# Moving the large SBUF buffers of an attention decode kernel to multiples of 4 KB

## Chip, cores and metric

The kernel runs on one core of one Trainium2 chip. The metric is the device time of one execution in microseconds.

## The reference, cut to what matters

One token, 32 query heads, 8 KV heads, 65536 cached keys of 128 dimensions, all bf16:

```python
q = (x @ wq) as 32 heads of 128
scores = einsum(q, k) * 128 ** -0.5        # k_cache, v_cache: [1, 8, 65536, 128]
o = einsum(softmax(scores), v)
h = x + o.reshape(1, 1, 4096) @ wo         # x is layer-normed before wq
h2 = h + (sigmoid(g) * u) @ w_down         # g, u = norm(h) @ w_gate, w_up (512 x 1792)
```

The two caches are 128 MB (MiB) each, so the kernel reads 282.33 MB (10^6 bytes) per call and computes little on each byte.

## The kernel before

K and V come in blocks of 4 MB: 128 partitions, one contiguous row of 32 KB for each. They land in four slots of one tensor, `ring`. VectorE transposes K from `ring` into `ktw`; TensorE makes scores from `ktw` and the output from the V slots. `ktw` is used again for `wo`, and the slots for the feed-forward weights. Allocation is in the order of the calls, from the bottom of SBUF up:

```python
SLOT = T * DH                                  # 16384 bf16 = 32 KB a partition
ring = sb("ring", [128, NSLOT * SLOT], bf16)   # the first tensor of the kernel
ktw = sb("ktw", [128, NKT * CH + WH], bf16)
P_sb = sb("P_sb", [128, 4 * 512], bf16)
# ... [cut: some 50 smaller tensors]

order = [("wq", 0)]
order += [("K", b) for b in range(NR)]
for b in range(NR, NB):
    order += [("K", b), ("V", b - NR)]
# ... [cut: the last V blocks and the weights]
for ld in order:
    k, b = ld
    s = slot_of[ld]
    dst = slot_ap(s)
    deps = [freed(prev[ld])]                   # the slot's last reader
    # ... [cut: weights]
    src = cache[0, h, r * BLK:(r + 1) * BLK, :].rearrange("(p t) d -> p (t d)", t=T)
    dma("sp", lambda e, d=dst, sr=src: e.dma_start(d, sr), ..., deps, f"{k}{b}")
```

In the built program some constants lie below `ring`, which therefore starts at byte 16512 of each partition; `ktw` starts at 147584. Both are 128 bytes past a multiple of 4096.

## Time and profile before

Median 660.75 us of 3 runs (660.71 to 660.75).

| what | value | where |
|---|---|---|
| load queue | 99.7% of the time of 16 DMA engines | page, queues |
| rate, 100 to 600 us | 432 GB/s | DMA view of that stretch |
| TensorE, VectorE busy | 64%, 53% | page, engines |
| 32 KB packets, 140 to 580 us | 1213 to 1224 ns, mean 1217.0 | the trace's DMA records |

The page of the kernel before:

```profile
span 659.3 us, 6111 instructions
PE 418.7 (64%) x2315; PEld 73.3 (11%) x1547; DVE 349.7 (53%) x439; ACT 42.9 (7%) x114; POOL 3.6 (1%) x17
...
DMA  9999999999999999999999999999999999999998
...
q1 hardware_dynamic: 10658, 282.33, 99.7%
...
DMA 36%; DVE 28%; PE 28%; issue 6%; ACT 1%; SPq 0%; DVEq 0%
...
L430 PE MATMUL PS<-ktw 128*128 128x512 bf16 x1024 | 298.2, 440 | 160.1 <-DVE ktw L510 156.3
L510 DVE STREAM_TRANSPOSE ktw<-ring 128x1024 f32<-128x1024 f32 x256 | 291.6, 1205 | 131.0 <-DMA ring<-in_A_k_cache_dram 131.0
...
ring<-in_A_k_cache_dram SPq DMA_DIRECT2D x32, 4096.0 KB, 29.3
ring<-in_A_v_cache_dram SPq DMA_DIRECT2D x31, 4096.0 KB, 26.9
```

The queue line (packets, MB, share) and the row of nines show DMA engines that never pause until the last slice. The chain of waits names VectorE and TensorE for over half of the span, but a load lands 27 to 29 us after its issue while 4 MB take 9.7 us at 432 GB/s: about three loads are queued at any time, and compute only decides when the next one joins (in the waits view the issues of loads, L364, wait 326.7 us for VectorE and 246.7 us for TensorE). VectorE's transposes wait 131 us in all for K to land.

The DMA view of the kernel before, 100 to 600 us (packets, MB and rate; then the load queue):

```profile
DMA packets 7408, 216.01 MB, mean 432 GB/s; under 512 B 816, under 2 KB 816, under 8 KB 816
...
q1 hardware_dynamic: 7408, 216.01, 100.4%
```

Over 100% means that the records of neighbouring packets of one engine overlap by a few ns. So the record's length is not quite the time a packet takes up. The better number is the period: 16 engines work side by side, and the start of the packet 16 places later, minus the start of this one, averaged over 140 to 580 us, is 1214.17 ns, 2.8 ns less than the mean record of 1217.0 ns. (The stretches given for packet records count from the trace's own zero, which lies about 11 us before the span that the views count from: 11.4 us in this run.)

### The profile page before, as it was taken

Reading aid. Unit: us, or ns where it says so; the run is one execution under the profiler, and the core shown is the slowest. Engines: PE = TensorE matmul, PEld = TensorE weight load, DVE = VectorE, ACT = ScalarE, POOL = GpSimd, SP = SyncE. Lnnn points to the kernel's source line nnn. Section 1 sums busy time; section 2 is a strip of 40 time slices with the busy share of each in tenths; the row PEclk is TensorE's granted clock in tenths of the full one; section 3 lists DMA queues with packets and bytes.
Section 4 is the critical chain, followed back from the end, with each engine's and each line's share of the span. In section 5 each row is a group of like instructions: output and inputs, shape, how many; then the busy total and the mean of one; then the engine's idle time right before and its main releaser. Section 6 shows DMA issues by size and latency. Waiting matters only on the chain.

```text
span 659.3 us, 6111 instructions
## 1 busy us (share of the span) xinstructions
PE 418.7 (64%) x2315; PEld 73.3 (11%) x1547; DVE 349.7 (53%) x439; ACT 42.9 (7%) x114; POOL 3.6 (1%) x17
## 2 busy tenths in 40 slices
PE   0688488548666585576765475764856668555846
PEld 0200011011000010010100110001100101001222
DVE  2299775547437665346555374465743565543202
ACT  1100200020000200020000200002000200002001
POOL 1000000000000000000000000000000000000000
PEclk9989699668887696776966779766878869667676
DMA  9999999999999999999999999999999999999998
GB/s 382 445 427 431 441 418 445 421 437 429 429 443 416 445 421 437 431 427 445 416 443 423 435 435 423 445 416 443 423 435 437 421 445 416 443 425 438 429 416 344
DMA packets 10802, 282.34 MB, mean 428 GB/s; under 512 B 1329, under 2 KB 1330, under 8 KB 1842
## 3 DMA queue, kind: packets, MB, share of 16 engines
q1 hardware_dynamic: 10658, 282.33, 99.7%
q10 hardware_dynamic: 144, 0.00, 0.0%
HBM read 282.33 MB, written 0.00 MB: 428 GB/s over the span
## 4 chain that ended last, share of the span: by engine, by line
DMA 36%; DVE 28%; PE 28%; issue 6%; ACT 1%; SPq 0%; DVEq 0%
DMA ring<-in_A_k_cache_dram 29%; PE PS L430 26%; DVE ktw L510 22%; DMA ring<-in_B_w_down_dram 4%; DVE M_sb L515 3%; DMA x_col<-in_A_x_dram 2%; DVE PT_sb L564 2%; ACT po_sb L598 1%; PE PS L548 1%; PE PS L541 1%; DVE gmj L543 0%; DVE gmrep L545 0%; PE PS L601 0%; PE PS L569 0%; DVE gm L539 0%
## 5 line engine op out<-in xcount | busy, mean ns | idle before, releaser
L430 PE MATMUL PS<-ktw 128*128 128x512 bf16 x1024 | 298.2, 440 | 160.1 <-DVE ktw L510 156.3
L510 DVE STREAM_TRANSPOSE ktw<-ring 128x1024 f32<-128x1024 f32 x256 | 291.6, 1205 | 131.0 <-DMA ring<-in_A_k_cache_dram 131.0
L430 PE MATMUL PS<-ring,PT_sb 128*32 x1024 | 83.2, 455 | 24.0 <-issue 13.5
L430 PEld LDWEIGHTS PS<-ktw 128*128 x256 | 26.9, 105 | 409.4 <-issue 256.5
L564 DVE STREAM_TRANSPOSE PT_sb<-P_sb 128x512 bf16<-128x512 bf16 x32 | 20.1, 684 | 53.5 <-PE PS L601 51.8
L550 ACT ACTIVATE negmax<-PS 128x1 f32<-128x1 f32 x8 | 1.4, 171 | 521.8 <-PE PS L548 521.8
L430 PEld LDWEIGHTS PS<-ring,PT_sb 128*32 x1024 | 25.4, 116 | 80.8 <-issue 76.1
L515 DVE TENSOR_REDUCE M_sb<-PS 128x1 f32<-128x512 f32 x32 | 19.9, 682 | 25.0 <-PE PS L430 25.0
L554 ACT ACTIVATE P_sb<-PS,negmax 128x512 bf16<-128x512 f32 x32 | 21.5, 685 | 0.3
L571 DVE TENSOR_REDUCE lsum<-PS 128x1 f32<-128x4 f32 x8 | 1.3, 162 | 29.9 <-PE PS L569 29.9
L541 PE MATMUL PS<-identf,gm 128*1 128x128 f32 x16 | 3.4, 301 | 16.9 <-DVE gm L539 16.9
L615 DVE TENSOR_TENSOR Lw<-O,blk_of 128x896 bf16<-128x896 bf16 (+1 forms) x2 | 1.4, 682 | 21.7 <-ACT O L605 21.7
L401 PE MATMUL PS<-st,onesf 128*128 128x2 f32 x4 | 1.2, 362 | 16.3 <-DVE st L400 16.3
L430 PE MATMUL PS<-ring,xz 128*8 x32 | 9.5, 470 | 2.3 <-issue 2.3
L598 ACT ACTIVATE po_sb<-PS,rl 128x512 bf16<-128x512 f32 x8 | 5.5, 687 | 53.6 <-PE PS L430 53.6
L430 PE MATMUL PS<-ktw,O 128*1 x26 | 7.5, 455 | 0.0
L548 PE MATMUL PS<-one_f,gmrep 1*128 1x1 f32 x16 | 4.2, 332 | 5.0 <-DVE gmrep L545 5.0
L475 DVE STREAM_TRANSPOSE qt<-qh 32x512 bf16<-32x512 bf16 x1 | 0.7, 700 | 11.0 <-ACT qh L472 11.0
L554 ACT ACTIVATION_READ_ACCUMULATOR P_sb<-PS,negmax 128x1 f32 x32 | 6.5, 203 | 0.0
L601 PE MATMUL PS<-sel_bf,po_sb 128*128 128x4 bf16 x32 | 2.1, 169 | 6.4 <-ACT po_sb L598 6.4
L416 DVE CAST hT<-x_col 128x4 f32<-128x4 bf16 x1 | 0.2, 170 | 10.8 <-DMA x_col<-in_A_x_dram 10.8
L660 DVE COPY yr<-PS 1x512 f32<-1x512 f32 x1 | 0.7, 679 | 8.1 <-PE PS L658 8.1
(82 smaller groups left out, 73.1 us busy)
## 6 DMA issues: line engine op xcount, KB each, us to landing
ring<-in_A_k_cache_dram SPq DMA_DIRECT2D x32, 4096.0 KB, 29.3
ring<-in_A_v_cache_dram SPq DMA_DIRECT2D x31, 4096.0 KB, 26.9
ring<-in_A_wq_dram SPq DMA_DIRECT2D x1, 4096.0 KB, 12.5
ktw<-in_A_wo_dram SPq DMA_DIRECT2D x1, 3584.0 KB, 13.3
ring<-in_A_v_cache_dram SPq DMA_DIRECT2D x1, 3072.0 KB, 13.2
ring<-in_B_w_gate_dram SPq DMA_DIRECT2D x1, 1792.0 KB, 19.1
ring<-in_B_w_up_dram SPq DMA_DIRECT2D x1, 1344.0 KB, 21.9
ring<-in_A_v_cache_dram SPq DMA_DIRECT2D x1, 1024.0 KB, 15.3
```

Of the source, the lines that this page charges most:

```text
L430: return e.add_instruction(mybir.InstMatmult(name=nc.get_next_instruction_name(), engine=mybir.EngineType.PE, ins=[rhs, lhsT], outs=[e.low ...
L510: op("dve", lambda e, d=dst, sr=src: e.transpose(d, sr), deps, f"T{b}.{c}", to="T")
L515: op("dve", lambda e, u=u: e.tensor_reduce(M_sb[:, u % 4:u % 4 + 1], ps(u % NS, 0, 512), AX.X, ALU.max), [f"S{b}.{NC - NR + k}"], f"mx{u}" ...
L541: op("pe", lambda e: e.matmul(ps(MISC, 0, 128, 0, 1), lhsT=gm[:, :], rhs=identf[:, :], start=True, stop=True), [f"gm{h}"], f"gmT{h}", to="Q")
L548: op("pe", lambda e: e.matmul(ps(MISC, 128, 129), lhsT=gmrep[0:1, :], rhs=one_f[0:1, 0:1], start=True, stop=True), [f"gmrep{h}"], f"neg{h}")
L550: op("act", lambda e: e.activation(negmax[:, k:k + 1], ps(MISC, 128, 129), AF.Copy, scale=-att_scale), [f"neg{h}"], f"negmax{h}")
L554: op("act", lambda e, b=b: e.activation(P_sb[:, (b % 4) * 512:(b % 4 + 1) * 512], ps(b % NS, 0, 512), AF.Exp, bias=negmax[:, k:k + 1], sca ...
L564: op("dve", lambda e, b=b: e.transpose(PT_sb[:, (b % 4) * 512:(b % 4 + 1) * 512], P_sb[:, (b % 4) * 512:(b % 4 + 1) * 512]), [f"E{b}", f"o ...
L571: op("dve", lambda e: e.tensor_reduce(lsum[:, :], ps(MISC, 132, 136), AX.X, ALU.add), [f"l{h}"], f"ls{h}", to="D")
L598: op("act", lambda e: e.activation(po_sb[:, :], ps(PO, 0, 512), AF.Copy, scale=rl[:, :]), [f"PV{NR * h + NR - 1}", f"rl{h}"], f"po{h}", to ...
L601: op("pe", lambda e, t=t: e.matmul(ps(OX, 0, 4), lhsT=po_sb[:, t * 128:(t + 1) * 128], rhs=sel_bf[:, 8 * t:8 * t + 8:2], start=(t == 0), s ...
L615: op("dve", lambda e: e.tensor_tensor(Lw[i][:, :].rearrange("p (j c) -> p j c", j=n), bass.AP(tensor=O2, offset=j0, ap=[[NQ, 128], [1, n], ...
```

## The change

The intent: the large DMA writes should start on a multiple of 4 KB in SBUF. Small tensors that came later now come first and fill the space up to byte 20480.

```diff
+        gsel = sb("gsel", [128, 128], fp32)
+        hz = sb("hz", [128, 128], fp32)
+        # ... [cut: 10 more small tensors, moved up from below]
+        blk_of = sb("blk_of", [128, 128 // RW], bf16)
         ring = sb("ring", [128, NSLOT * SLOT], bf16)
         ktw = sb("ktw", [128, NKT * CH + WH], bf16)
+        assert nc.lookup_mloc(ring).addr % 4096 == nc.lookup_mloc(ktw).addr % 4096 == 0
         P_sb = sb("P_sb", [128, 4 * 512], bf16)
         # ... [cut: the same small tensors taken out here and further down]
```

`ring` now starts at 20480 and `ktw` at 151552. Every engine has the same instructions in the same order.

More of the change, by code (lines that the diff above doesn't have):

```diff
@@ L236, in sb @@
             return es.enter_context(nc.sbuf_tensor(name, shape, dt))
+        gsel = sb("gsel", [128, 128], fp32)
+        hz = sb("hz", [128, 128], fp32)
+        identf = sb("identf", [128, 128], fp32)
+        onesf = sb("onesf", [128, 128], fp32)
+        lsel = sb("lsel", [128, 128], fp32)
+        iota_i = sb("iota_i", [128, 128], i32)
+        ident = sb("ident", [128, 128], bf16)
+        scr = sb("scr", [1, 64], fp32)
+        sel_f = sb("sel_f", [128, 32], fp32)
+        sel_bf = sb("sel_bf", [128, 32], bf16)
+        O2 = sb("O2", [128, NQ], bf16)
+        O3 = sb("O3", [128, NQ], bf16)
+        blk_of = sb("blk_of", [128, 128 // RW], bf16)
         ring = sb("ring", [128, NSLOT * SLOT], bf16)
         ktw = sb("ktw", [128, NKT * CH + WH], bf16)
+        assert nc.lookup_mloc(ring).addr % 4096 == nc.lookup_mloc(ktw).addr % 4096 == 0
         P_sb = sb("P_sb", [128, 4 * 512], bf16)
@@ L243, in bass_sequential_preLN__gqa_block_cached__glu_gated_glu__decode_kernel @@
         yr = sb("yr", [1, 512], fp32)
-        gsel = sb("gsel", [128, 128], fp32)
-        hz = sb("hz", [128, 128], fp32)
-        scr = sb("scr", [1, 64], fp32)
         po_sb = sb("po_sb", [128, 512], bf16)
-        O2 = sb("O2", [128, NQ], bf16)
-        ident = sb("ident", [128, 128], bf16)
-        identf = sb("identf", [128, 128], fp32)
-        onesf = sb("onesf", [128, 128], fp32)
-        lsel = sb("lsel", [128, 128], fp32)
-        iota_i = sb("iota_i", [128, 128], i32)
-        sel_f = sb("sel_f", [128, 32], fp32)
-        sel_bf = sb("sel_bf", [128, 32], bf16)
         one_f = sb("one_f", [1, 1], fp32)
@@ L284, in bass_sequential_preLN__gqa_block_cached__glu_gated_glu__decode_kernel @@
         W0 = NKT * CH
-        O3 = sb("O3", [128, NQ], bf16)
         Lw = [sb(f"Lw{i}", [128, n * DH // RW], bf16) for i, (_, n) in enumerate(WO)]
         row_of = sb("row_of", [128, RW], bf16)
-        blk_of = sb("blk_of", [128, 128 // RW], bf16)
         head_of = sb("head_of", [128, 4], fp32)
```

## The prediction

> **What bounds the kernel.** The DMA stream. The page's queue part shows the load queue busy for 99.7% of 16 engines' span, moving 282.33 MB; its engine part has PE at 64%, DVE at 53%, ACT at 7%. From 100 to 600 us the DMA view shows 432 GB/s and 100.4% busy (packets overlap by a few ns); K and V loads land a median 29.6 and 27.1 us after issue, about three 4 MB loads deep, so the queue never runs dry. The chain of waits is labelled DMA 36%, DVE 28%, PE 28%, but its DVE and PE steps run while loads are in flight; they pace the issues, not the bytes. Only about 2 us at the end (down-projection, cast, store) follow the last weight's landing.
>
> **What the change does.** Every engine runs the same instructions in the same order; only allocations move. In the built program the ring goes from byte 16512 to 20480 of each partition, the K-transpose/weight buffer from 147584 to 151552: both started 128 bytes past a multiple of 4 KB and now start on one. Every large load writes one of these two at offsets that are multiples of 512 bytes, so every large write was 128 bytes off a 256-byte boundary and is now on it. HBM sources don't move. No engine instruction should take a different time.
>
> **Cost.** DMA packets in the trace, lowest usual durations: 84 ns (2 KB), 140 (3.5), 159 (4), 404 (10.5), 535 (14), 912 (24), 1062 (28), 1213 (32 KB; median 1218). The slope from 2 to 32 KB is (1213-84)/30 = 37.6 ns per KB, 435 GB/s over 16 engines[...]. What remains is a constant of about 8.5 ns a packet, not growing with the number of 4 KB pages, plus up to 5 ns that look like contention. So no per-page penalty is visible for 4 KB alignment to remove; only the constant can shrink.
>
> [...] whether writes pay, this trace doesn't show. If they do, [...] at 37.6 ns per KB an estimate of 4.7 ns a packet, half of the constant. An engine carries about 592 large packets (9473/16): 592 x 4.7 = 2.8 us, all on the critical path. Upper bound: 282.33 MB at 435 GB/s take 649 us against 655 us from first to last load packet, 6 us; in the steady part 432 to 435 is 0.7%, about 4.6 us. Lower bound: nothing.
>
> **Prediction.** 660.75 - 2.6 = 658.2 us; range 655.4 to 661.0. Faster by over 2%: 3%; within 2%: 96%; slower by over 2%: 1%.
>
> **What would show it.** 32 KB packets drop from 1213/1218 ns to about 1208/1213; 432 GB/s in the middle becomes 433 to 434; small packets lose the same 4 to 5 ns, not a proportional share. DVE transposes stay at 1205 ns, score matmuls at 440 ns. If packets keep their durations, the time stays at 660.7.
>
> **What would make it wrong.** A rate above 435 GB/s: then the slope itself held a cost of misaligned writes[...], and the gain could pass 1 to 2%. Or compute slowed by changed SBUF neighbours, which the slack would mostly hide.

The forecast's sum came to 2.8 us, of which it wrote down 2.6: 592 packets of an engine times 4.7 ns, which is 128 bytes at 37.6 ns per KB, the slope in the trace.

## The result

Median 658.56 us of 6 runs (658.14 to 659.41), against 660.65 us (660.47 to 660.75) of the kernel before in the same rounds: ratio 0.997, 95% interval 0.9957 to 0.9982. A ratio here is the mean time of one kernel's fast runs over that of the other's of the same rounds, so it is not quite the ratio of the medians quoted. The interval is clear of 1.

The page of the changed kernel (line numbers are one higher):

```profile
span 657.1 us, 6111 instructions
PE 420.5 (64%) x2315; PEld 74.1 (11%) x1547; DVE 349.7 (53%) x439; ACT 42.9 (7%) x114; POOL 3.6 (1%) x17
...
DMA  9999999999999999999999999999999999999998
...
q1 hardware_dynamic: 10658, 282.33, 99.7%
...
L431 PE MATMUL PS<-ktw 128*128 128x512 bf16 x1024 | 299.9, 442 | 157.4 <-DVE ktw L511 153.6
L511 DVE STREAM_TRANSPOSE ktw<-ring 128x1024 f32<-128x1024 f32 x256 | 291.6, 1205 | 128.0 <-DMA ring<-in_A_k_cache_dram 128.0
...
ring<-in_A_k_cache_dram SPq DMA_DIRECT2D x32, 4096.0 KB, 28.7
ring<-in_A_v_cache_dram SPq DMA_DIRECT2D x31, 4096.0 KB, 26.4
```

The queue is as full as before, with the same packets and bytes, in a span 2.2 us shorter. Engine instructions took nearly the same time; VectorE waits 3 us less for K. (In this profile the chain of waits breaks off after the last 2% of the span, so it can't be set beside the one before.)

The DMA view of the changed kernel, 100 to 600 us:

```profile
DMA packets 7424, 216.53 MB, mean 433 GB/s; under 512 B 816, under 2 KB 816, under 8 KB 816
...
q1 hardware_dynamic: 7424, 216.53, 100.3%
```

More bytes passed in the same 500 us. What happened is clearest in the trace's records of the 32 KB packets, counted by length for 140 to 580 us:

```
                  up to 1213 ns   1214-1216   1217-1219   1220-1224   longer   mean length   period
before                 923           1550        1944        1360       16      1217.0      1214.17 ns
changed               5824              0           0           0        0      1213.0      1210.14 ns
```

The shortest packets are no shorter than before. The spread above them has gone. The period fell by 4.03 ns a packet; an engine carries about 592 large packets (9473/16), and 592 x 4.03 ns = 2.4 us, against 2.1 us measured. (Device time also holds 1.3 us or more outside the span of instructions. Three of the six runs lost 0.5 to 1.0 us there beyond the other three, which may be part of the gap.)

One oddity of the kernel before: from 12.6 to 42.6 us of the span all 400 of its 32 KB packets took 1213 ns as well. The longer ones start near 46 us. The last four experiments take that up.

This profiled run of the changed kernel was the slowest of its six (659.41 us). Between 53 and 129 us of the span it has 94 packets of over 1230 ns; the run `pad4k` below, which has the same addresses for the large buffers, has none there. They add 0.3 us an engine, as much as this span is longer than that of the fastest run (657.1 against 656.8 us). The rest of the distance from 658.14 us lies outside the span: 2.3 us of device time are there in this run, 1.3 us in the fastest. Why is not known; neither is part of the effect.

### The profile page after: what moved, and what is told of

Read it like the earlier page. It is cut to its first block, busy times and chain, and to the rows that moved or that the text cites. A ratio compares the mean times of both kernels' runs of the same rounds, so it can differ in the third digit from the quotient of the medians.

```text
span 657.1 us, 6111 instructions
## 1 busy us (share of the span) xinstructions
PE 420.5 (64%) x2315; PEld 74.1 (11%) x1547; DVE 349.7 (53%) x439; ACT 42.9 (7%) x114; POOL 3.6 (1%) x17
## 5 line engine op out<-in xcount | busy, mean ns | idle before, releaser
L511 DVE STREAM_TRANSPOSE ktw<-ring 128x1024 f32<-128x1024 f32 x256 | 291.6, 1205 | 128.0 <-DMA ring<-in_A_k_cache_dram 128.0
```

The source lines that it names most:

```text
L511: op("dve", lambda e, d=dst, sr=src: e.transpose(d, sr), deps, f"T{b}.{c}", to="T")
```

## The experiments

The theory (A) is that the start address of the large writes is the whole cause, and that the DMA engines pay for it by themselves. The rivals: 4 KB matters, or only a smaller boundary (B); the moved small tensors did it (C); misaligned writes collide with the engines' accesses to SBUF (E). Eleven kernels ran. The first four shared one chip and the runs of the kernel before, and so did the next three and the last four. The medians of before in these groups were 660.70, 660.81 and 660.82 us.

### pad4k: alignment without the new order

```diff
+        sb("pad", [128, 1984], bf16)           # 3968 bytes, unused
         ring = sb("ring", [128, NSLOT * SLOT], bf16)
```

> The kernel before with one unused 3968-byte tensor ahead of the ring: ring and K-transpose buffer at multiples of 4 KB, small tensors in their old order. Theory A (the start address of the large writes is the whole cause): ratio to before 0.997, about 658.4 us, all 32 KB packets at 1213 ns as in the changed kernel. Rival C (the moved small tensors did it): 660.7 us, packets at a median of 1218 ns.

Measured: 658.61 us, ratio 0.9966 (0.9952 to 0.998); all 5822 packets of the stretch at 1213 ns. The whole gain is there with every small tensor in its old order. The DMA view, 100 to 600 us:

```profile
DMA packets 7431, 216.76 MB, mean 434 GB/s; under 512 B 816, under 2 KB 816, under 8 KB 816
```

### front128: the new order without alignment

```diff
         blk_of = sb("blk_of", [128, 128 // RW], bf16)
+        sb("pad", [128, 64], bf16)             # 128 bytes, unused
         ring = sb("ring", [128, NSLOT * SLOT], bf16)
-        assert nc.lookup_mloc(ring).addr % 4096 == nc.lookup_mloc(ktw).addr % 4096 == 0
+        assert nc.lookup_mloc(ring).addr % 4096 == nc.lookup_mloc(ktw).addr % 4096 == 128
```

> The changed kernel's order of tensors with a 128-byte unused tensor ahead of the ring, so that both large buffers are again 128 bytes past a multiple of 4 KB. Theory A: 660.7 us, ratio 1.000, packets spread over 1213 to 1224 ns with a mean of 1217 in the steady part. Rival C: about 658.5 us.

Measured: 660.64 us, ratio 0.9999 (0.9985 to 1.0013); packets with a mean of 1217.0 ns, period 1214.19 ns. Theory C falls: the new order alone gives nothing. The same view shows the packets and bytes of the kernel before:

```profile
DMA packets 7408, 216.01 MB, mean 432 GB/s; under 512 B 816, under 2 KB 816, under 8 KB 816
```

### pad256: is it 4 KB?

The kernel before with a 128-byte `pad` ahead of the ring, so that the buffers are 256 bytes past a multiple of 4 KB.

```diff
+        sb("pad", [128, 64], bf16)             # 128 bytes, unused
         ring = sb("ring", [128, NSLOT * SLOT], bf16)
```

> The kernel before with 128 unused bytes ahead of the ring: large buffers at 256 past a multiple of 4 KB (a multiple of 256, not of 512). Theory A1 (what counts is a 256-byte boundary): the whole gain, ratio 0.997, packets all 1213 ns. Rival B (4 KB, or 512 bytes, count): no gain, 660.7 us, packets with a mean of 1217.

Measured: 658.35 us, ratio 0.9962 (0.9948 to 0.9975); all 5814 packets at 1213 ns. 4 KB is not needed, nor 512 bytes; a multiple of 256 gives all of it, for 128 bytes of space. It ties with the changed kernel (658.56 us in other rounds) and is simpler. The same view again:

```profile
DMA packets 7429, 216.70 MB, mean 433 GB/s; under 512 B 816, under 2 KB 816, under 8 KB 816
```

### off64 and off32: does the distance from the boundary matter?

The same edit with a `pad` of 192 or 160 bytes, so that the buffers are 64 or 32 bytes past a 256-byte boundary.

```diff
+        sb("pad", [128, 96], bf16)             # off64: 192 bytes; off32: [128, 80], 160 bytes
         ring = sb("ring", [128, NSLOT * SLOT], bf16)
```

Both expectations put the theory that the cost goes with the bytes past the boundary against a cost that is the same for any start off it.

> The kernel before with 192 unused bytes ahead of the ring: large buffers 64 bytes past a 256-byte boundary. Theory A1[...]: half of the extra of 128 bytes, so packets about 2 ns over 1213 on average and about 659.6 us. Theory A2 (any start off 256 bytes costs the same): 660.7 us.[...]

> The kernel before with 160 unused bytes ahead of the ring: large buffers 32 bytes past a 256-byte boundary[...]. [...] a quarter of the extra of 128 bytes, about 1 ns a packet, 659.1 us. If any start off 256 bytes costs the same: 660.7 us.[...]

| start past 256 bytes | time (ratio, interval) | mean packet | period | period over aligned |
|---|---|---|---|---|
| 0 (`pad256`) | 658.35 (0.9962, 0.9948-0.9975) | 1213.0 | 1210.14 | 0 |
| 128 (`front128`) | 660.64 (0.9999, 0.9985-1.0013) | 1217.0 | 1214.19 | 4.05 ns |
| 64 (`off64`) | 660.83 (1.0000, 0.9986-1.0013) | 1216.8 | 1214.26 | 4.12 ns |
| 32 (`off32`) | 661.12 (1.0005, 0.9988-1.0022) | 1217.8 | 1215.26 | 5.12 ns |

The cost is not in proportion to the bytes past the boundary. 64 costs what 128 costs; 32 costs a little more in the packet records, and its time (0.3 us over its own before) is within the interval. So the prediction's estimate (the bytes past the boundary at 37.6 ns per KB), by which 32, 64 and 128 bytes would cost about 1.2, 2.4 and 4.7 ns, is refuted as an account of these writes, although its number for 128 bytes was nearly right. Why 64 and 128 bytes cost the same (4.12 and 4.05 ns), and 32 bytes 1 ns more, no run tells. Starts more than 128 bytes past the boundary were not run.

### loads128 and loads0: without the compute

Wrong results (zeros): the same loads to the same addresses, each waiting only for the load before it in its slot.

```diff
-            return {"wq": "q", "K": f"F{b}", "V": f"PV{b}"}[k]      # the slot's last reader
+            return "wq" if k == "wq" else f"{k}{b}"                 # the load itself has landed
 # ... all matmuls, transposes and activations taken out; y_sb set to zero and stored at the end
```

`loads128` has the addresses of the kernel before, `loads0` those of the changed kernel.

> Loads alone (wrong result on purpose, output zeros): the same loads to the same addresses as the kernel before, each waiting only for the load before it in its slot to land; no other engine works. Theory D (the DMA engines pay for the misaligned write by themselves): packets with a mean of about 1217 ns, as with the compute. Rival E (the extra is contention between misaligned writes and the engines' SBUF accesses): all packets 1213 ns.

> Loads alone as the run before it, to the changed kernel's addresses (multiples of 4 KB). Both theories: packets at 1213 ns. D: about 2 us (0.3%) faster than the loads alone at 128 bytes; E: the same time.

Measured: 659.73 us (659.58 to 660.1) at 128 bytes and 657.43 us (657.21 to 657.69) aligned, 2.30 us apart on one chip, with mean packets of 1217.0 and 1213.0 ns as in the full kernels. The windows view of `loads128` shows that nothing else worked (columns: VectorE and GpSimd busy, granted clock, DMA share, GB/s):

```profile
core 0: us, DVE busy (x) POOL busy (x), PEclk, DMA share, GB/s
...
100.00:600.00 500.00, 0.00 (x0) 0.00 (x0) 1.00 1.00 432
```

And the same view of the kernel before, whose stretch moved its bytes at the same rate with both big engines at work:

```profile
core 0: us, PE busy (x) PEld busy (x) DVE busy (x) ACT busy (x) POOL busy (x), PEclk, DMA share, GB/s
...
100.00:600.00 500.00, 320.83 (x1733) 49.14 (x1101) 274.23 (x322) 28.11 (x78) 0.00 (x0) 0.77 1.00 432
```

Theory E falls: the extra is there in full with no engine touching SBUF. (What takes the extra time was not tested.) The pair also shows how far the kernel is bound by its loads. The full kernel before is 1.1 us slower than its loads alone (660.81 to 659.73, same chip).

The DMA view of `loads0`, 100 to 600 us:

```profile
DMA packets 7431, 216.76 MB, mean 434 GB/s; under 512 B 816, under 2 KB 816, under 8 KB 816
```

### half128 and half0: per packet or per byte?

Loads alone again, each 4 MB load as two of 2 MB, so 16 KB rows: twice the packets, the same bytes.

```diff
-                    dma("sp", lambda e, d=dst, sr=src: e.dma_start(d, sr), ..., deps, f"{k}{b}")
+                    for i in range(2):
+                        d2, s2 = (ap[:, i * SLOT // 2:(i + 1) * SLOT // 2] for ap in (dst, src))
+                        dma("sp", lambda e, d=d2, sr=s2: e.dma_start(d, sr), ..., deps if i == 0 else (), ...)
```

> Loads alone at 128 bytes past 4 KB, each 4 MB K or V load as two of 2 MB (16 KB rows, so twice the packets, the same bytes). Theory F (the extra is a constant per misaligned packet): the gap to the aligned twin doubles from 2.3 us to about 4.5 us, and packets are about 4 ns over the aligned ones on average. Rival G (the extra goes with the bytes): the gap stays at 2.3 us, packets 2 ns over.

> Loads alone at multiples of 4 KB in 16 KB rows: all packets about 610 ns. Against the loads alone in 32 KB rows (657.4 us) about 512 more packets an engine times the aligned constant of about 5 ns, so about 660 us.

Measured: 664.77 us (664.49 to 664.99) and 660.07 us (659.92 to 660.23), 4.70 us apart: about twice the 2.30 us of whole rows. Periods are 611.93 and 607.84 ns, so 4.09 ns a packet, as with 32 KB (4.03). An engine now carries about 1096 large packets (63 loads were split, 8 more packets of an engine for each), and 1096 x 4.09 ns = 4.5 us. So the extra is a constant per misaligned packet for these two sizes. The DMA views, 100 to 600 us, of `half128` and then of `half0`:

```profile
DMA packets 14712, 214.25 MB, mean 429 GB/s; under 512 B 1635, under 2 KB 1635, under 8 KB 1635
```

```profile
DMA packets 14794, 215.63 MB, mean 431 GB/s; under 512 B 1633, under 2 KB 1633, under 8 KB 1633
```

The aligned pair also splits a packet's time in two. 16 KB more cost 1210.14 - 607.84 = 602.3 ns, 435.2 GB/s over 16 engines; and each packet has a constant of 2 x 607.84 - 1210.14 = 5.5 ns beside it. This constant is there with and without alignment.

### drain128 and drain0: why did the first packets cost nothing?

In the kernel before, apart from the first few, the packets of each engine stay at 1213 ns until about the 36th. With 16 KB rows the longer ones also set in between the 32nd and the 38th packet (the first 8 are still of 32 KB), so after fewer bytes. In the run `loads128` they set in between the 28th and the 38th. That suggested a lag which builds up per packet. Theory H takes it that each misaligned packet costs about 4 ns from the first one on, although the first 30-odd records don't show it; rival I, that the extra begins later. The test empties the queue after every four loads (32 packets of an engine):

```diff
             deps = [freed(prev[ld])]
+            at = order.index(ld)
+            if k in "KV" and at % 4 == 1:
+                deps.append(freed(order[at - 1]))      # the load issued just before has landed
```

> Loads alone at 128 bytes, but every fourth load waits until the load issued just before it has landed, so the queue runs empty 16 times. It asks why the first 35 or so packets of each engine stayed at 1213 ns. Theory H[...]: with a drain after every 32 packets of an engine nearly all packets are at 1213 ns. Rival I (the extra begins with time, with the mix of K and V, or with the engines' phases): packets average 1217 ns from 70 us on, apart from the one or two right after a drain.

> The same drains at multiples of 4 KB: packets 1213 ns, apart from those right after a drain. Theory H: although the packets of both drained kernels look alike, this one is still about 2 us faster, as the lag is paid at each landing. Rival I: if packets look alike, so do the times.

Measured: 700.14 us (699.84 to 700.62) and 697.56 us (696.53 to 698.29), both longer for the 16 pauses. From the third packet after a pause on, the mean by place is 1212.9 to 1213.0 ns in both, over the 15 stretches of 32 packets. So the misaligned packets look free, right through the time in which they averaged 1217 ns without pauses. But the misaligned kernel is still 2.58 us slower. The page of `drain128` and then of `drain0`:

```profile
span 699.3 us, 115 instructions
...
q1 hardware_dynamic: 10658, 282.33, 95.3%
```

```profile
span 696.0 us, 115 instructions
...
q1 hardware_dynamic: 10658, 282.33, 95.6%
```

The misaligned one spends a slightly smaller share in packets: most of the difference sits between them. The packet records show where. From the last packet before a pause to the first one after it, the 15 pauses that follow 32 packets of each engine take 1443 ns on average in `drain128` (1421 to 1493) and 1310 ns in `drain0` (1281 to 1343). The 133 ns between them fit 32 x 4.03 = 129 ns. The one pause that follows only 8 packets takes 1264 and 1238 ns, 26 ns apart, where 8 x 4.03 ns would be 32. Together the pauses hold 2.0 of the 3.3 us by which the two spans differ. (The rest was not traced; the runs of `drain0` alone spread over 1.8 us.)

This is what theory H forecast: records alike (1212.9 to 1213.0 ns in both), and yet the times 2.58 us apart. The pauses fit a cost of about 4 ns a packet from the first packets on (26 ns after 8 of them, 133 ns after 32), which with drains shows in the pause and not in a packet's record. Rival I falls. Why the records of the first 30-odd packets hide it was not shown.

## Why the prediction was right, point by point

- **"The DMA stream" bounds the kernel:** right. Loads alone take 659.73 us of 660.81, and the changes of the packets' period came out as time: 2.4 us expected from it and 2.1 to 2.4 measured for 32 KB rows, 4.5 and 4.7 for 16 KB rows. (For `off32` the 1 ns more was too little to tell.)
- **Only the addresses matter, not the moved tensors:** right (`pad4k`, `front128`).
- **"No per-page penalty is visible for 4 KB alignment to remove":** right. 256 bytes are enough (`pad256`), and the slope of 435 GB/s did not change: the lowest usual records of 2 and 32 KB packets are 84 and 1213 ns before and after.
- **"592 x 4.7 = 2.8 us, all on the critical path":** that it is a constant per misaligned packet was right (4.03 ns at 32 KB, 4.09 at 16). The term measured 4.03 ns, so 2.4 us, and 2.1 us arrived; the number written down (2.6 instead of 2.8, for no reason that it gives; time 658.2 us) was 0.4 us off the measured 658.56.
- **"Half of the constant", with packets going "from 1213/1218 ns to about 1208/1213":** this step failed. The floor of about 8.5 ns above the slope stayed (1213 ns before and after). What went was the part set aside as "up to 5 ns that look like contention". It was no contention with the engines: it is there with all of them idle (mean 1217.0 ns in `loads128`). The loss was booked under the wrong term, and only because both terms were about 5 ns did the sum come out.
- **"... an estimate of 4.7 ns a packet":** near the measured 4.03 ns for 128 bytes by chance. The estimate takes the cost to go with the bytes past the boundary, and for these writes it does not: 32 and 64 bytes cost 5.12 and 4.12 ns.
- **"Small packets lose the same 4 to 5 ns":** partly. 14 KB packets lost 4.8 ns on average (539.8 to 535.0), 28 KB 4.3, 4 KB 2.9 (161.9 to 159.0), 2 KB 1.4. These come in the last loads and are lengths of records, which can hide a delay (1213 ns in both drained kernels, whose times are 2.58 us apart); why the smallest lose less was not tested.
- **"432 GB/s becomes 433 to 434":** right, 433 (434 in `loads0`). VectorE's transposes stayed at 1205 ns; score matmuls went from 440 to 442, off the critical path.

The slope limited the gain, as stated: between 16 and 32 KB packets it is 435.2 GB/s here. With the aligned period at 433.2 GB/s (16 x 32768 B / 1210.14 ns), no more than half a per cent was left to win there, an estimate that takes the slope of these packets as fixed.

## What to carry to other kernels

When a queue of loads is full from end to end, price a change by the packet: fit the packet's time as a slope times its bytes plus a constant, see how near the rate is to the slope already (432 of 435 GB/s here before the change), and multiply what may change in the constant by the number of packets. Put the SBUF side of large loads on a multiple of 256 bytes; it costs a pad of less than 256 bytes, gave here 4.03 to 4.09 ns a packet (128 bytes past the boundary before), and so came to 2.30 us with rows of 32 KB and 4.70 us with rows of 16 KB. Do not call a regular spread of lengths in a record contention before you have run the same transfers alone: here the spread stayed.
